# A windowed attention and MLP kernel: the first two batches rebuilt, the global rows split per head, scores and PV reordered

## Chip, cores and metric

One core of a Trainium2 chip. The metric is the device time of one execution in microseconds; the kernel before has a median of 496.06 us over 3 runs (493.28 to 496.7).

## The reference

Shapes: 8 batches, 8 heads, 576 positions, head size 64; model width 512, hidden width 2048; all inputs fp32. Attention with a window of 32 to either side, plus 8 global positions that see all and are seen by all, then a residual MLP with a token mix:

```python
scores = scale * np.matmul(q, k.transpose(0, 1, 3, 2))
mask = (np.abs(pos[:, None] - pos[None, :]) <= 32) | is_global[:, None] | is_global[None, :]
attn = softmax(where(mask, scores, -1e9))        # per batch and head
x = np.matmul(attn, v)                           # heads side by side: (8, 576, 512)
tok = np.einsum('ts,bsd->btd', w_tok, alpha1 * x + beta1)
u = x + lam * tok
out = u + lam * (np.maximum((alpha2 * u + beta2) @ w_ch1, 0.0) @ w_ch2)
```

## The kernel before

The kernel is written out by hand: every engine executes its instructions in the order in which the program emits them, and DMA queues belong to the engine that issues (SP, ScalarE's or POOL's; POOL's convert types).

**A batch of attention.** Heads go in four pairs (hp). `sc_unit(b, hp, u)` is a third of a pair's band scores: three matmuls KT × QP (144 or 128 columns) into a score bank (there are two, banks 3 and 4), Exp on ScalarE to E; the third unit also makes on VectorE PGQ (queries at global positions) and PT (masked band). QP holds Q padded to two halves per pair, with 8 global query columns at each even block of 64; `qpad` and `gcols` copy these in on VectorE from QT and QGT, and `gcols` also places the gathered global keys in KGP. `gk_half` makes the scores of the global keys against all queries (EG, and with the mask GM the rows G). `gq_pv` computes, for the global queries, PGQ × Ve and turns it into RG by three VectorE operations (lines 308 to 310). `pv_x` and `pv_y` compute five tiles of 128 positions: G × RG (one matmul, 130 columns for two heads), then per head PT × Ve and PT × Vo (65 columns each: 64 and the sum); `norm` divides on VectorE into XR, and XL = XR · LA1 follows (on VectorE for batch 0, on POOL for others; LA1 is alpha1 · lam).

**Token mix and MLP.** `tok_tile` multiplies wtT (transposed w_tok) with XL; `finish_u` adds x on VectorE, POOL makes UB = u · alpha2, and a DMA transpose on SP's queue writes it into UT. The MLP runs over nine groups of four tiles (an "S" tile joins the last 64 positions of two batches): 64 matmuls with W1, Relu on ScalarE into HT, 64 matmuls with W2, of 512 columns each: 128 slots. W2 is scaled by lam when it is loaded (`w2_scale`, lines 711 to 715, in group 0), so an output is one VectorE addition, x = bank + x (line 483), and a DMA.

**The order.** `weave` lays attention of batch g+1 over slots 2 to 90 of group g and its token mix over 94 to 114; loads of batch g+2 start at slots 2 to 60 (`prefetch`, K and Q as bf16 by POOL's queue in 256-byte runs), their DMA transposes into KT and QT at 60 to 100 (`xbars`), `qpad` and `gcols` at 116 to 127. Within a batch `attention` (line 437) orders units so:

```python
a = [gk_half(b, 0), gk_half(b, 1)]
...
a += [s[0], w[0], s[1], w[1], w[2], s[2], w[3], w[4]]   # s: scores of pair i, w: PV of pair i-1
if i < HP:
    a.append(gq_pv(b, i))
```

**The first batch** runs ahead of the groups (lines 506 to 706): K and Q are loaded as fp32 in runs of 1 KB (`ld_b0`), cast, and transposed by TensorE one pair at a time between score units; then PV, row sums of w_tok (times ones, for beta1), token mix, bias1 (W1 × beta2). Batch 1 there takes the way of the later batches: `prefetch(1)` at line 674, `xbars(1)`, `qpad`, `gcols` at lines 717 to 721, directly before group 0. POOL multiplies LA1 by lam at line 647, after the loads of line 634.

Of the kernel before, what the change touches and what calls it, by code (L numbers as in the profile page):

```python
# [47 lines left out]
def _consts():  # L48
    p = np.arange(P)
    c16 = np.zeros((P, 64 + 576 + 130), np.float16)  # L50
# [4 lines left out]
    for a in range(2):  # L55
        c16[:, 640 + 65 * a : 705 + 65 * a] = (ab == a)[:, None]
    c16[64:, 640:770] /= GSC
    c16[80, 640:770] = 0
    c16[80, [704, 769]] = EPS_B
    c32 = np.zeros((P, 176), np.float32)  # L60
    c32[:, 48:176] = np.eye(P)
# [727 lines left out]
```

## Time and profile before

| | |
|---|---|
| median of 3 runs | 496.06 us |
| the profiled execution: its time, its span | 495.06 us, 493.3 us |
| TensorE busy | 387.7 us (79%) |
| VectorE busy | 241.4 us (49%) |
| POOL busy | 218.8 us (44%) |
| ScalarE busy | 155.7 us (32%) |
| mean granted TensorE clock (of full speed) | 0.952 |
| moved by DMA | 52.63 MB |

Busy time says how long an engine had an instruction in it; matmuls overlap in a pipeline, so TensorE's share is not a share of its peak. The idle time before an instruction, and what ended it, say more: a stage ends with the wait that ends last in it.

### The profile page before, as it was taken

To read this page: it belongs to the slowest core of one execution; us is meant where nothing else is said; L and a number is where in the kernel's file an instruction comes from. 1 tells how busy PE (TensorE), PEld (TensorE's weight loads), DVE (VectorE), ACT (ScalarE), POOL (GpSimd) and SP (SyncE) were. 2 spreads that over 40 slices of the span, in tenths; PEclk is the share of its full clock that TensorE was granted. 3 is DMA by queue.
4 is the path that set the end of the run, shared out by engine and by line. 5 is a ranking of instruction groups with operands and counts; after the bars stand their busy time and mean duration, and the time that the engine had idled before them with its cause. 6 is when DMAs were issued, how large, how long until landed. Compare 5 with 4: busy or idle time off the path is not lost.

```text
span 493.3 us, 7444 instructions
## 1 busy us (share of the span) xinstructions
PE 387.7 (79%) x2727; PEld 204.8 (42%) x2727; DVE 241.4 (49%) x697; ACT 155.7 (32%) x275; POOL 218.8 (44%) x270
## 2 busy tenths in 40 slices
PE   0336640657897889978998898899889888999995
PEld 0225420333444544544455444444544454444442
DVE  7666620576654556456544555655464555301101
ACT  1242100443105610750076035402640461062440
POOL 6459161266345834854656467546454122500000
PEclk9998585687999999999999999999999999999999
DMA  9999749499269945992599369949965200221102
GB/s 210 211 208 156 34 102 182 90 200 167 42 130 144 114 59 122 154 111 54 122 179 82 68 159 132 72 102 145 142 46 139 76 2 23 64 55 43 44 21 64
DMA packets 179008, 52.63 MB, mean 107 GB/s; under 512 B 166806, under 2 KB 171802, under 8 KB 178972
## 3 DMA queue, kind: packets, MB, share of 16 engines
q0 software_dynamic: 107264, 20.20, 52.0%
q1 hardware_dynamic: 69964, 30.59, 30.0%
q10 hardware_dynamic: 1744, 1.38, 1.0%
q8 instruction: 21, 0.34, 0.3%
q14 instruction: 15, 0.12, 0.1%
HBM read 39.38 MB, written 9.44 MB: 99 GB/s over the span
## 4 chain that ended last, share of the span: by engine, by line
PE 44%; DVE 23%; DMA 10%; issue 8%; SPq 5%; ACT 5%; POOL 3%; POOLq 0%; DVEq 0%; ACTq 0%
PE bank L119 43%; DVE PT L292 4%; DVE QP L216 4%; ACT E L280 3%; DVE PGQ L287 3%; DMA UT<-UB 3%; DMA KG<-in_k_dram,hidx 2%; DVE RG L310 2%; SPq L208 2%; SPq L211 2%; DVE XR L338 2%; DVE RGt L309 2%; DMA XR<-in_moe_w_ch_dram 1%; DVE SR L338 1%; POOL UB L401 1%
## 5 line engine op out<-in xcount | busy, mean ns | idle before, releaser
L119 PE MATMUL bank<-UT,W 128*128 128x512 bf16 x576 | 160.7, 387 | 9.2 <-DMA UT<-UB 7.6
L119 PE MATMUL bank<-W,HT 128*128 128x512 bf16 x576 | 142.5, 379 | 0.0
L470 ACT ACTIVATE HT<-bank,bias 128x512 bf16<-128x512 f32 x144 | 98.9, 687 | 85.3 <-PE bank L119 82.5
L119 PEld LDWEIGHTS <-HT 128*128 128x128 bf16 x576 | 52.0, 98 | 50.6
L361 POOL TENSOR_TENSOR XL<-XR,LA 128x384 bf16<-128x384 f32 x28 | 27.9, 998 | 87.8 <-DVE XR L338 54.8
L401 POOL TENSOR_TENSOR UB<-XR,A 128x512 bf16<-128x512 f32 x32 | 40.5, 1267 | 58.9 <-DMA UT<-UB 25.8
L119 PEld LDWEIGHTS <-W 128*128 128x128 bf16 x640 | 50.8, 99 | 35.9 <-issue 11.0
L119 PE MATMUL bank<-RG,G 128*128 128x130 f16 x160 | 36.0, 226 | 32.7 <-DVE RG L310 32.7
L280 ACT ACTIVATE E<-bank 128x416 f16<-128x416 f32 (+1 forms) x96 | 48.0, 511 | 40.5 <-PE bank L119 40.3
L256 ACT ACTIVATE EG<-bank 128x288 f16<-128x288 f32 (+2 forms) x16 | 6.6, 410 | 168.4 <-PE bank L119 168.3
L119 PEld LDWEIGHTS <-PT 128*128 128x128 f16 x576 | 33.9, 101 | 53.7 <-issue 39.8
L483 DVE TENSOR_TENSOR XR<-bank,XR 128x512 f32<-128x512 f32 x32 | 21.9, 685 | 54.9 <-PE bank L119 54.9
L119 PE MATMUL bank<-XL,wtT 128*128 128x512 bf16 x180 | 44.9, 379 | 0.8 <-ACT wt4o L688 0.8
L335 DVE RECIPROCAL rd<-bank 128x6 f32<-128x6 f32 (+2 forms) x96 | 16.6, 173 | 54.7 <-PE bank L119 54.1
L119 PE MATMUL bank<-Ve,PT 128*128 128x65 f16 x320 | 40.6, 199 | 0.0
L398 DVE TENSOR_TENSOR XR<-bank,XR 128x512 f32<-128x512 f32 x32 | 22.1, 691 | 36.1 <-PE bank L119 36.1
L200 POOL DMA_DIRECT2D Ve<-in_v_dram x40 | 34.7, 876 | 4.4 <-DVE Ve L504 2.2
L119 PEld LDWEIGHTS <-KT 128*128 128x128 bf16 x288 | 25.7, 104 | 23.7 <-issue 5.4
L119 PE MATMUL bank<-QP,KT 128*128 128x144 bf16 (+1 forms) x288 | 34.2, 234 | 1.4 <-ACT E L280 1.4
L216 DVE COPY QP<-QT 64x576 bf16<-64x576 bf16 x56 | 25.0, 446 | 18.7 <-DMA QT<-Qb 18.1
L287 DVE TENSOR_TENSOR PGQ<-E,gqm 128x80 f16<-128x80 f16 x64 | 16.8, 302 | 33.3 <-ACT E L280 33.2
L119 PE MATMUL bank<-Vo,PT 128*128 128x65 f16 x256 | 33.1, 198 | 0.0
(109 smaller groups left out, 394.3 us busy)
## 6 DMA issues: line engine op xcount, KB each, us to landing
out_dram<-XR SPq DMA_DIRECT2D x32, 256.0 KB, 2.2
Vo<-Ve SPq DMA_DIRECT2D x16, 260.0 KB, 3.8
XR<-in_moe_w_ch_dram POOLq DMA_DIRECT2D x8, 512.0 KB, 4.5
Kb<-in_k_dram POOLq DMA_DIRECT2D x28, 128.0 KB, 6.2
Qb<-in_q_dram POOLq DMA_DIRECT2D x28, 128.0 KB, 6.0
Ve<-in_v_dram POOLq DMA_DIRECT2D x24, 128.0 KB, 4.4
W<-in_moe_w_ch_dram POOLq DMA_DIRECT2D x4, 512.0 KB, 16.4
Ve<-in_v_dram POOLq DMA_DIRECT2D x16, 96.0 KB, 4.7
```

Of the source, the lines that this page charges most:

```text
L119: nc.tensor.matmul(out=o, lhsT=l, rhs=r, start=st, stop=sp, skip_group_check=True)
L200: nc.gpsimd.dma_start(out=Ve[b % 2][r0 : r0 + hi - lo, c, :, 0:D], in_=v[b, :, lo:hi, :].rearrange("h p d -> p h d"))
L216: nc.vector.tensor_copy(out=QP[r, hp, a, :, 0:64], in_=QT[r, hp, 0:S].rearrange("p (t j) -> p t j", j=64))
L280: nc.scalar.activation(out=e[:, UOFF[u] : UOFF[u + 1]], in_=ps[:, 0:off], func=AF.Exp, bias=0.0, scale=0.125)
L287: nc.vector.tensor_tensor(out=pg[:, :, c0 : c0 + 16].rearrange("p c (a g) -> p c a g", a=2), in0=gq_in, in1=gq_m, op=ALU.mult)
L292: nc.vector.tensor_tensor(out=bass.AP(pt.tensor, pt.offset + 64 + 128 * par, [p0, [256, n], [1216, 2], [1, 64]]), in0=bass.AP(e.tensor, e. ...
L335: nc.vector.reciprocal(out=rt[r0:r1, 0:m], in_=pv[:, :, 64:65].rearrange("p i o -> p (i o)"))
L361: xl_eng(b).tensor_tensor(out=XL[b % 2][:, 0:3, 128 * hp : 128 * hp + 128], in0=xo, in1=bass.AP(l.tensor, l.offset, [l.ap[0], [0, 3], [1, ...
L398: nc.vector.tensor_tensor(out=x, in0=ps, in1=x, op=ALU.add)
L401: nc.gpsimd.tensor_tensor(out=ub, in0=x, in1=A2, op=ALU.mult)
L470: nc.scalar.activation(out=HT[:, ec, :], in_=st["ps"], func=AF.Relu, bias=bias1[:, ec : ec + 1], scale=1.0)
L483: nc.vector.tensor_tensor(out=x, in0=ps, in1=x, op=ALU.add)
```

## The change

- **Loads.** Batch 1's K and Q come like batch 0's, as fp32 in 1 KB runs (`ld_kq`, `ld_tail`) on SP's queue, half of them behind wtT's DMA transposes. Batch 0's loads go nearly all to SP. The identity for transposes is an own constant.
- **Batch 0** transposes all pairs first, then scores, with fills and mask arithmetic hung between units (`hooks`); QP, XL4, V and other fills go to POOL ahead of the gather; XL of batch 0 goes to POOL; the product of LA1 and lam goes from POOL to VectorE.
- **Batch 0's UT** is made by TensorE: four fp32 transposes per tile, VectorE multiplies by alpha2 out of the bank (`late`). No UB and no DMA transpose for these four tiles.
- **Batch 1** is cast (K on POOL, Q on VectorE) and transposed by TensorE inside group 0: `first_attention(1)` lies over slots 4 to 112, its token mix over 112 to 124. `tr_pair` uses the two score banks.
- **W2** is loaded straight as bf16, unscaled, four DMAs; each output becomes ot = bank · lam, x = ot + x on VectorE.
- **Global rows**: G gets one copy per head of a pair, so G × RG becomes two matmuls of 65 columns; RG is one ScalarE copy with a scale and one VectorE operation on 32 partitions.
- **Order**: a batch's scores of the first pair come ahead of the global keys; s0 and s1 come ahead of the first PV tile; the gather's arithmetic and transposes are spread over slots 44, 56 and 60; `norm` takes one reciprocal for two tiles in `pv_y`.

The core of the diff (other functions keep their computation):

```diff
+    def g_rows():
+        for lo, hi, o in ((0, 512, 0), (512, S, 576)):
+            n = hi - lo
+            e = EG[:, lo:hi]
+            nc.vector.tensor_tensor(
+                out=G[:, :, o : o + n], in0=bass.AP(e.tensor, e.offset, [e.ap[0], [0, 2], [1, n]]), in1=GM[:, :, lo:hi], op=ALU.mult
+            )
...
+    def gk_pair(hp, pss):
+        def f():
+            for hf, t0, nt in ((0, 0, 4), (1, 4, 5)):
+                for a in range(2):
+                    o = pss[hf][:, 0 : 64 * nt].rearrange("p (t j) -> p t j", j=64)
+                    mm(o, KGP[:, hp, :], QP[:, hp, a, t0 : t0 + nt, 0:64], hp == 0 and a == 0, hp == HP - 1 and a == 1)
+            if hp == HP - 1:
+                for hf, q0, n in ((0, 0, 256), (1, 256, 320)):
+                    nc.scalar.activation(out=EG[:, q0 : q0 + n], in_=pss[hf][:, 0:n], func=AF.Exp, bias=0.0, scale=0.125)
+                g_rows()
+        return (0.6, f)
...
-            m2 = C16[:, 640:770]
-            nc.vector.tensor_tensor(out=rg, in0=ps[:, 0:130], in1=m2, op=ALU.mult)
-            nc.vector.tensor_tensor(out=RGt[96:128], in0=ps[96:128, 0:130], in1=m2[96:128], op=ALU.mult)
-            nc.vector.tensor_tensor(out=rg[96:128], in0=RGt[96:128], in1=rg[96:128], op=ALU.subtract)
+            nc.scalar.activation(out=rg, in_=ps[:, 0:130], func=AF.Copy, bias=0.0, scale=C32[:, 36:37])
+            nc.vector.scalar_tensor_tensor(
+                out=rg[96:128], in0=ps[96:128, 0:130], scalar=1.0 / GSC, in1=rg[96:128], op0=ALU.mult, op1=ALU.subtract
+            )
...
         gs = slice(128 * i, 128 * i + 128) if i < 4 else (slice(576, 704) if par == 0 else slice(512, 640))
-        mm(o, G[:, gs], RG[hp % 2], True, False)
         pt = PT[hp % 2]
         for a in range(2):
             oa = o[:, 65 * a : 65 * a + 65]
+            mm(oa, G[:, a, gs], RG[hp % 2][:, 65 * a : 65 * a + 65], True, False)
...
-        return nc.vector if b == 0 else nc.gpsimd
+        return nc.gpsimd
...
+        g, j = PLACE[t]
+        js = slice(128 * j, 128 * j + 128)
+        if t[0] == 0:
+            def tail():
+                for cc in range(4):
+                    nc.tensor.transpose(out=ps[:, 128 * cc : 128 * cc + 128], in_=x[:, 128 * cc : 128 * cc + 128], identity=ident)
+                ab = bass.AP(a2c.tensor, a2c.offset, [a2c.ap[0], [1, 4], [0, 128]])
+                nc.vector.tensor_tensor(out=UT[g % 2][:, :, js], in0=ps.rearrange("p (c t) -> p c t", c=4), in1=ab, op=ALU.mult)
+            late.append(tail)
+            return
         ub = UB[nub[0] % 2]
         nub[0] += 1
         nc.gpsimd.tensor_tensor(out=ub, in0=x, in1=A2, op=ALU.mult)
-        g, j = PLACE[t]
-        nc.sync.dma_start_transpose(out=UT[g % 2][:, :, 128 * j : 128 * j + 128], in_=ub)
+        nc.sync.dma_start_transpose(out=UT[g % 2][:, :, js], in_=ub)
...
-        a = [gk_half(b, 0), gk_half(b, 1)]
+        a = []
         for i in range(HP + 1):
             s = [sc_unit(b, i, u) for u in range(3)] if i < HP else []
             w = pv_x(b, i - 1) + pv_y(b, i - 1) if i > 0 else []
-            if not w:
-                a += s
+            if i == 0:
+                a += s + [gk_half(b, 0), gk_half(b, 1)]
             elif not s:
                 a += w
             else:
-                a += [s[0], w[0], s[1], w[1], w[2], s[2], w[3], w[4]]
+                a += [s[0], s[1], w[0], w[1], w[2], s[2], w[3], w[4]]
...
-                    nc.vector.tensor_tensor(out=x, in0=ps, in1=x, op=ALU.add)
+                    ot = OT[nout[0] % 2]
+                    nout[0] += 1
+                    nc.vector.tensor_tensor(out=ot, in0=ps, in1=LAM, op=ALU.mult)
+                    nc.vector.tensor_tensor(out=x, in0=ot, in1=x, op=ALU.add)
...
+    def cast_k(hp, copy):
+        copy(out=KB0[:, :, 128 * hp : 128 * hp + 128].rearrange("p j (a d) -> p a j d", a=2), in_=KST[:, 2 * hp : 2 * hp + 2, :, :])
+    def cast_q(b, hp, copy):
+        copy(out=QB0[b][:, :, 128 * hp : 128 * hp + 128].rearrange("p j (a d) -> p a j d", a=2), in_=QST[:, 2 * hp : 2 * hp + 2, :, :])
+    def tr_pair(b, hp):
+        def f():
+            kt = KT[b % 2]
+            if b == 0:
+                psq, psk = [banks[i].bitcast(BF16) for i in ((0, 1) if hp % 2 == 0 else (2, 6))]
+            else:
+                psq, psk = sc_ps().bitcast(BF16), sc_ps().bitcast(BF16)
+            hs = slice(128 * hp, 128 * hp + 128)
+            for ps, st_ in ((psq, QB0[b]), (psk, KB0)):
+                for j in range(4):
+                    nc.tensor.transpose(out=ps[:, 128 * j : 128 * j + 128], in_=st_[:, j, hs], identity=identb)
+            if hp == 0:
+                pst = (banks[7] if b == 0 else pv_ps()).bitcast(BF16)
+                for i in range(4):
+                    nc.tensor.transpose(out=pst[:, 128 * i : 128 * i + 128], in_=TSB[:, 128 * i : 128 * i + 128], identity=identb)
+            nc.scalar.copy(out=kt[:, hp, 32:544].rearrange("p (t j) -> p t j", j=4), in_=psk[:, 0:512].rearrange("p (j t) -> p t j", j=4))
+            for a, eng in ((0, nc.vector.tensor_copy), (1, nc.scalar.copy if b == 0 else nc.vector.tensor_copy)):
+                r = slice(64 * a, 64 * a + 64)
+                eng(
+                    out=QP[r, hp, a, 0:8, 0:64].rearrange("p t (u j) -> p t u j", j=4),
+                    in_=psq[r, 0:512].rearrange("p (j t u) -> p t u j", j=4, t=8),
+                )
+            if hp == 0:
+                tv = pst[:, 0:512].rearrange("p (i t) -> p i t", i=4)
+                nc.scalar.copy(out=kt[:, :, 544:608], in_=tv[:, :, 0:64])
+                for a in range(2):
+                    r = slice(64 * a, 64 * a + 64)
+                    nc.vector.tensor_copy(out=QP[r, :, a, 8, 0:64], in_=tv[r, :, 64:128])
+        return (1.2, f)
+    def first_attention(b):
+        pss = [None, None]
+        def hold():
+            pss[0], pss[1] = pv_ps(), pv_ps()
+        def s(hp):
+            return [sc_unit(b, hp, u) for u in range(3)]
+        tail = s(0) + [gk_pair(0, pss)] + s(1) + [gk_pair(1, pss), gk_pair(2, pss), gk_pair(3, pss), gq_pv(b, 0)]
+        if b == 0:
+            a = [tr_pair(b, hp) for hp in range(HP)] + [(0.0, lambda: gcols(b)), (0.0, hold)] + tail
+        else:
+            a = [tr_pair(b, 0), (0.0, lambda: gcols(b)), (0.0, hold), tr_pair(b, 1)] + tail[0:4] + [tr_pair(b, 2)] + tail[4:8] + [tr_pair(b, 3)] + tail[8:]
+        for hp in range(HP):
+            s3 = s(hp + 2) if hp + 2 < HP else []
+            g1 = [gq_pv(b, hp + 1)] if hp + 1 < HP else []
+            a += s3[0:2] + pv_x(b, hp) + pv_y(b, hp) + g1 + s3[2:3]
+        return a
...
+    for c in range(5):
+        load_v(0, c)
...
+    def b0_weights():
+        for t_, src in ((LA1, alpha1), (LAM, lam), (A2, alpha2)):
+            nc.sync.dma_start(out=t_, in_=src.unsqueeze(0).to_broadcast([P, DM]))
+        for r in (64, 0):
+            nc.sync.dma_start(out=LB[r : r + 1, :], in_=beta1.unsqueeze(0))
+        nc.sync.dma_start(out=abr[0:4, :], in_=beta2.rearrange("(c p) -> c p", p=P))
+        nc.sync.dma_start(out=abr[4:8, :], in_=alpha2.rearrange("(c p) -> c p", p=P))
+        nc.vector.tensor_tensor(out=LA1, in0=LA1, in1=LAM, op=ALU.mult)
...
+    def b0_wtok():
+        for tcn in range(5):
+            c0 = 128 * tcn if tcn < 4 else 576
+            nc.sync.dma_start_transpose(out=wtT[:, :, c0 : c0 + 128], in_=WTB[:, tcn, :])
+        nc.sync.dma_start(out=wt4o[64:128, :], in_=wtT[0:64, 4, :])
+    def b1_fills():
+        for c in range(5):
+            load_v(1, c)
+        ld_w1(2)
+        ld_w1(3)
+    def b1_kq(h0, h1):
+        ld_kq(k, KST, nc.sync, 1, h0, h1)
+        ld_kq(q, QST, nc.sync, 1, h0, h1)
+    def cast0(hp):
+        cast_k(hp, nc.scalar.copy)
+        cast_q(0, hp, nc.vector.tensor_copy)
+    def b0_gather():
+        for i in range(2):
+            gather_x(i)
+            gather_tr(0, i)
...
+    hooks = {
+        0: [lambda: cast0(2)],
+        1: [b0_arith, lambda: cast0(3)],
+        3: [b0_gather],
+        4: [b0_masks, lambda: copy_vo(0), b0_weights],
+        9: [b0_gm, b1_fills, lambda: b0_beta(0)],
+        10: [lambda: ld_tail(k, nc.sync, 1, 0), lambda: ld_tail(q, nc.sync, 1, 64), lambda: b1_kq(0, 4), b0_wtok, lambda: b1_kq(4, 8)],
+    }
+    cast0(1)
+    for i, (w, f) in enumerate(early):
+        f()
+        for h in hooks.get(i, []):
+            h()
...
+    for hp in range(HP):
+        cast_k(hp, nc.gpsimd.tensor_copy)
+        if hp == 1:
+            for blk in range(4):
+                nc.gpsimd.dma_start(out=W2[:, 4 * blk : 4 * blk + 4, :], in_=w_ch2[512 * blk : 512 * blk + 512, :].rearrange("(c p) e -> p c e", p=P))
+    b0_beta(1)
...
+    for i, (w, f) in enumerate(token_mix(0)):
+        f()
+        if i > 0:
+            late[i - 1]()
+    late[3]()
...
+    nc.vector.tensor_copy(out=TSB, in_=TST)
+    for hp in range(HP):
+        cast_q(1, hp, nc.vector.tensor_copy)
...
-        if g == 0:
-            slots[0] += [lambda: w2_load(0), lambda: w2_load(1)]
-            for blk in range(8):
-                slots[8 + 7 * blk].append(lambda blk=blk: w2_scale(blk))
         if nb < NB:
             if nb % 2 == 0:
-                def tr(pr=nb // 2):
-                    gather_tr(pr)
-                timed([lambda pr=nb // 2: gather(pr)], slots, 1, 2)
-                timed([tr], slots, 40, 41)
+                pr = nb // 2
+                slots[1].append(lambda pr=pr: gather(pr))
+                slots[44] += [lambda: gather_x(0), lambda: gather_x(1)]
+                slots[56].append(lambda pr=pr: gather_tr(pr, 0))
+                slots[60].append(lambda pr=pr: gather_tr(pr, 1))
...
-        parts = [(attention(g + 1), 2, 90), (token_mix(g + 1), 94, 114)] if g + 1 < NB else []
+        if g == 0:
+            parts = [(first_attention(1), 4, 112), (token_mix(1), 112, 124)]
+        elif g + 1 < NB:
+            parts = [(attention(g + 1), 2, 90), (token_mix(g + 1), 94, 114)]
```

## Rows read from the trace of the kernel before

**Rows 1.** Stages: start:end, length; busy us per engine; TensorE clock, DMA share, GB/s

```profile
66.90:89.10 22.20, 1.01 (x2) 0.14 (x2) 3.98 (x12) 0.00 (x0) 7.58 (x8) 0.58 0.91 168
89.10:150.20 61.10, 48.67 (x314) 24.89 (x314) 37.44 (x99) 17.01 (x30) 30.35 (x38) 0.87 0.80 123
...
196.40:246.10 49.70, 43.67 (x317) 22.87 (x318) 27.24 (x83) 16.68 (x30) 30.36 (x37) 1.00 1.01 110
```

**Rows 2.** Timeline of TensorE: start us, us, instruction [idle before <-releaser]

```profile
89.11 1.14 PE L119 MATMUL bank<-QT,KGP 128*128 128x288 bf16 x4 [13.83 <-DVE KGP L222]
```

**Rows 3.** Timeline of SP's queue, first and last of ten transposes

```profile
70.61 1.26 SPq L208 DMA_TRANSPOSE KT<-Kb  x1
...
82.57 1.22 SPq L211 DMA_TRANSPOSE QT<-Qb  x1
```

**Rows 4.** Groups of TensorE by line, 246.1 to 291.3: busy, mean ns | idle before

```profile
L119 PE MATMUL bank<-RG,G 128*128 128x130 f16 x20 | 4.4, 219 | 2.8 <-DVE RG L310 2.8
...
L119 PE MATMUL bank<-Ve,PGQ 128*128 128x130 f16 x20 | 1.8, 222 | 1.0 <-DVE PGQ L287 1.0
```

**Rows 5.** The same view, 291.3 to 340.9

```profile
L119 PE MATMUL bank<-RG,G 128*128 128x130 f16 x20 | 4.4, 219 | 3.4 <-DVE RG L310 3.4
...
L241 PE MATMUL bank<-C,QGx 128*128 128x128 f32 x1 | 0.3, 330 | 0.7 <-DVE QGx L239 0.7
```

**Rows 6.** Timeline of TensorE in a steady group

```profile
273.94 0.22 PE L119 MATMUL bank<-RG,G 128*128 128x130 f16 x1 [1.26 <-DVE RG L310]
...
291.17 0.66 PE L119 MATMUL bank<-QT,KGP 128*128 128x288 bf16 x4 [0.69 <-DVE KGP L222]
```

**Rows 7.** Timeline of all engines, the first 40 us

```profile
8.79 2.59 POOL L200 DMA_DIRECT2D Ve<-in_v_dram  x3
...
16.40 0.44 DVE L239 TENSOR_SCALAR KGx<-KG,C 128x64 f32<-128x64 f32 x2 [2.05 <-DMA KG<-in_k_dram,hidx]
...
18.11 0.53 SPq L204 DMA_DIRECT2D Vo<-Ve  x1
...
19.96 0.55 SPq L634 DMA_DIRECT2D LAM<-in_moe_lam_dram  x1
...
25.41 12.64 SPq L645 DMA_TRANSPOSE wtT<-HT  x5
...
29.51 1.26 POOL L647 TENSOR_TENSOR LA<-LA,LAM 128x512 f32<-128x512 f32 x1 [8.39 <-DMA LAM<-in_moe_lam_dram]
...
31.02 1.89 DVE L292 TENSOR_TENSOR PT<-E,mask 128x640 f16<-128x640 f16 x2
...
35.30 0.61 PE L576 MATMUL bank<-identb,UT 128*128 128x128 bf16 x4 [0.32 <-ACT UT L569]
```

**Rows 8.** Timeline of TensorE, batch 0's PV and token mix

```profile
41.55 0.22 PE L119 MATMUL bank<-RG,G 128*128 128x130 f16 x1 [1.49 <-DVE RG L310]
41.60 0.19 PE L119 MATMUL bank<-Ve,PT 128*128 128x65 f16 x1
41.63 0.19 PE L119 MATMUL bank<-Vo,PT 128*128 128x65 f16 x1
...
55.73 0.27 PE L119 MATMUL bank<-RG,G 128*128 128x130 f16 x1 [2.66 <-DVE RG L310]
...
60.82 4.48 PE L119 MATMUL bank<-XL,wtT 128*128 128x512 bf16 x20 [0.80 <-ACT wt4o L688]
```

**Rows 9.** Groups by line over the span

```profile
L713 DVE TENSOR_TENSOR W<-XR,LAM 128x512 bf16<-128x512 f32 x16 | 10.9, 725 | 1.9 <-DMA XR<-in_moe_w_ch_dram 1.9
L310 DVE TENSOR_TENSOR RG<-RGt,RG 32x130 f16<-32x130 f32 x32 | 10.8, 336 | 1.1
...
L308 DVE TENSOR_TENSOR RG<-bank,C 128x130 f16<-128x130 f32 x32 | 9.1, 285 | 0.4
```

**Rows 10.** Timeline of VectorE at the start of a steady group

```profile
291.03 0.30 DVE L228 COPY QP<-QGT 128x160 bf16<-128x160 bf16 x2
...
296.39 0.82 DVE L292 TENSOR_TENSOR PT<-E,mask 128x640 f16<-128x640 f16 x2
```

More of the change, by code (lines that the diff above doesn't have):

```diff
@@ L54, in _consts @@
     ab = (p % 16) // 8
[L55 to L61, printed above, removed]
+    oh = ((p >= 64) & (p < 80)) | ((p >= 96) & (p < 112))
+    c32 = np.zeros((P, 40), np.float32)
     c32[:, 0:9] = 64 * np.arange(9)[None, :] - 32 + p[:, None]
@@ L394 @@
     nub = [0]
+    late = []
     def finish_u(t, ps):
@@ L633 @@
-    for t_, src in ((LA1, alpha1), (LAM, lam), (A2, alpha2)):
-        nc.sync.dma_start(out=t_, in_=src.unsqueeze(0).to_broadcast([P, DM]))
-    for r in (64, 0):
-        nc.sync.dma_start(out=LB[r : r + 1, :], in_=beta1.unsqueeze(0))
-    nc.sync.dma_start(out=b2r, in_=beta2.rearrange("(c p) -> c p", p=P))
-    fill(XL4[0], 0.0, nc.gpsimd)
-    fill(XL4[1], 0.0, nc.gpsimd)
-    fill(ones, 1.0, nc.gpsimd)
-    fill(wtT[:, :, 512:576], 0.0, nc.gpsimd)
-    fill(wt4o, 0.0, nc.gpsimd)
-    for tcn in range(5):
-        c0 = 128 * tcn if tcn < 4 else 576
-        nc.sync.dma_start_transpose(out=wtT[:, :, c0 : c0 + 128], in_=WTB[:, tcn, :])
@@ L646, with ld_w1 @@
-    nc.sync.dma_start(out=wt4o[64:128, :], in_=wtT[0:64, 4, :])
-    nc.gpsimd.tensor_tensor(out=LA1, in0=LA1, in1=LAM, op=ALU.mult)
-    for par, r in ((0, 64), (1, 0)):
-        nc.gpsimd.tensor_tensor(out=XL4[par][r : r + 1, :], in0=LB[r : r + 1, :], in1=LAM[r : r + 1, :], op=ALU.mult)
+    def ld_w1(blk):
+        es = slice(512 * blk, 512 * blk + 512)
+        nc.gpsimd.dma_start(out=W1[:, :, es], in_=w_ch1[:, es].rearrange("(c p) e -> p c e", p=P))
+    ld_w1(0)
+    ld_w1(1)
+    nc.vector.tensor_copy(out=identb, in_=ident)
@@ new lines, in b0_beta @@
+    def b0_beta(par):
+        for par, r in ((0, 64), (1, 0))[par : par + 1]:
+            nc.gpsimd.tensor_tensor(out=XL4[par][r : r + 1, :], in0=LB[r : r + 1, :], in1=LAM[r : r + 1, :], op=ALU.mult)
+    def b0_wtok():
[8 more added lines that the diff above has]
+        ld_w1(3)
@@ new lines @@
+    cast0(1)
[3 more added lines that the diff above has]
+            h()
+    psr, psr2 = pv_ps(), pv_ps()
+    for sc in range(5):
+        mm(psr, ones, wtT[:, sc, 0:512], sc == 0, sc == 4)
+    for sc in range(5):
+        mm(psr2[:, 0:64], ones, wtT[:, sc, 576:640], sc == 0, sc == 4)
+    nc.scalar.copy(out=wtT[64:65, 4, 0:512], in_=psr[64:65, :])
+    nc.scalar.copy(out=wtT[64:65, 4, 576:640], in_=psr2[64:65, 0:64])
+    nc.scalar.copy(out=wt4o[0:1, 0:512], in_=psr[0:1, :])
@@ new lines @@
+    nc.scalar.copy(out=wt4o[0:1, 576:640], in_=psr2[0:1, 0:64])
+    for hp in range(HP):
[4 more added lines that the diff above has]
+    b0_beta(1)
+    psb = pv_ps()
+    nc.tensor.transpose(out=psb[:, 0:8], in_=abr, identity=ident[0:8, 0:8])
+    nc.vector.tensor_copy(out=b2c, in_=psb[:, 0:4])
```

329 lines of the change are left out of this document (129 added, 200 removed).

## The prediction

> **What bounds the kernel now.** I read the table of stages first, cut where groups of the MLP end [rows 1]. In the steady part TensorE is busy 43.67 us of a 49.7 us group, but in the 22.2 us between 66.9 and 89.1 it has two matmuls, at a mean granted clock of 0.58 (mostly the lower of its two levels, 1.2 GHz); group 0 then takes 61.1 us at 0.87. So there are two things to look at: the hole before group 0, and what is left idle in each later group.
>
> TensorE's timeline shows how the hole ends [rows 2]: after 13.83 us for KGP, the first instruction of batch 1's attention goes at 89.11, and the rest of group 0 stands behind it. What came late is on SP's queue [rows 3]: ten DMA transposes of batch 1's K and Q, the first at 70.61, the last ending at 83.79, about 1.3 us each, behind four of batch 0's UT. VectorE's Q padding and KGP follow them.
>
> In a steady group the waits are short and repeat. From 246.1 to 291.3 they are 2.8 us for RG and 1.0 for PGQ [rows 4]; the next group, with a shared tile and a gather, has 3.4 for RG and 0.7 for QGx [rows 5]. The timeline adds one for KGP at a group's start, 0.69 at 291.17, and the longest for RG, 1.26, ahead of a batch's last head pair [rows 6]. Over groups 1 to 6, three of either kind, that is 18.6 us for RG, 5.7 for PGQ, 1.4 for QGx and, with five such waits of 0.7 to 1.0, 4.0 for KGP: 29.7 us. They end on the order of VectorE's queue, not on its throughput.
>
> **Part 1, up to the start of group 0.** UT of batch 0 and K, Q of batch 1 no longer need those fourteen DMA transposes. I walk the new order:
> - POOL does its fills (QP's among them), then the gather, then all five V loads. Before, the gather was out at 8.79 and three V loads followed in 2.59 us, with Vo at 18.11 [rows 7]; two more ahead at 0.86 each and a little for the fills put Vo at 20 to 22. LA1 and LAM follow Vo on SP as before, LAM's issue at 22.5 in place of 19.96.
> - The product of LA1 and LAM moves from POOL to VectorE. Before, POOL sat idle 8.39 us for LAM and began at 29.51, 9.55 us after the issue [rows 7], with only its own later work behind it. After, VectorE waits until 22.5 + 9.5 = 32, and behind it stand the first pairs' PGQ and PT, GM and G. The casts and transposes should be done when the gather is in (16.4 before [rows 7], say 17 now); its transposes and column copies take 4 us, the masks 3: VectorE is there at 24. So this is a new wait of 8 us; bounds 0 (LAM early) and 15.
> - From 32: LA1 0.6, PGQ and PT of two pairs 2.2 (0.3 + 0.82 each), GM 1.4, G 1.0: the first PV near 37, against 41.55 [rows 8].
> - Head pairs came every 4.7 us (41.55 to 55.73 is three) [rows 8], with VectorE full. Of that XL (1.1 us) goes to POOL, RG shrinks from three operations of 0.285 to 0.336 us [rows 9] to one of 0.3 behind ScalarE's copy, one reciprocal (0.2) goes: 2.8 us of work, 3.2 with round trips. The last PV ends at 37 + 3 × 3.2 + 1.5 = 48.
> - Row sums of w_tok and their copies took from 57.2 (55.73 and its 1.5 us) to 60.82: 3.5 us, so 51.5. Token mix 4.48 us [rows 8]; sixteen fp32 transposes, 2 to 4 us, I take 2; then the last tile's sum, four transposes and the product with alpha2, 2 us. Group 0 starts at **60**, bounds 52 and 67.
>
> POOL's four casts of K, the four W2 loads and b0_beta(1) stand behind XL there and are needed only inside group 0: W2 from slot 64 on, over 20 us later. Batch 1's K and Q loads stand on SP's queue behind Vo and the weights, half of them also behind wtT; they should land near 52.
>
> **Part 2, group 0.** The group from 196.4 to 246.1, with a shared tile too, takes 49.7 us with some 6 of waits, so 43.7 of work. Added: 36 bf16 transposes at 0.61 us for four [rows 7], start to start about 0.1 each: 3.6 us; the global keys from QP instead of QT, twice the columns, 1.0. Gone: W2's scaling on VectorE. Waits: four times a pair's transposes take both score banks, and the next user waits for ScalarE's and VectorE's copies out, 1.2 us each, 5 us (bounds 0 and 9); RG, 1.5. In all 55 us (49 to 60). Token mix ends at slot 124 instead of 114, so UT of batch 1 comes later: its last tile has about 4.3 us for the sum, POOL's product and a DMA transpose, which need 5 to 6. I put 1 us on group 1.
>
> Group 0 ends at 60 + 55 + 1 = 116 in place of 150.2: **34 us** gained.
>
> **Part 3, groups 1 to 6.** The order becomes s0, s1, PV, and the global keys come after the first pair's scores.
> - RG: 0.6 us of VectorE's chain and 0.2 of reciprocal go, and s1 ahead of PV gives 0.6 us more cover. Waits of 0.7 to 1.0 vanish; a batch's last pair has no s1, so 1.26 becomes 0.4 and its like in the other groups 0.7: 18.6 shrinks to about 4.
> - PGQ: the global keys now lie between, 5.7 goes to 0. QGx is spread over slots, 1.4 to 0. Behind ScalarE's copy of RG stand only Exp and Relu of later units.
> - Against it: the first scores need the global columns of QP, two copies of 0.30 us together which VectorE makes after KGP [rows 10], so 0.3 us later. And each output gets a second operation on VectorE, x = ot + x: a product of two fp32 SBUF operands took 725 ns [rows 9], 0.64 uncontended as I take it; tile 2's stands directly ahead of the Q pads. The wait of about 0.85 at a group's start becomes 1.75: 4.0 turns into 10.5 over six.
> - RG split per head: a 130-column matmul holds TensorE 50 to 55 ns, a 65-column one 31 (41.55, 41.60, 41.63) [rows 8]: 7 ns for each of 160, 1 us.
>
> 29.7 − (4 + 10.5) − 1 = **14 us** gained; bounds 8 and 21.
>
> **Part 4, the end.** The last output waits for the second operation: 0.6 us lost. In groups 7 and 8 the others lie beside matmuls.
>
> **Sum.** Profiled execution 495.06 (span 493.3): −34 − 14 + 0.6 = 447.7. The median of the runs, 496.06, is 1.0 above that execution; rounded, I say **448**.
>
> **A rule against it.** Two PT products took 1.89 us at 31.02 while POOL multiplied, against 0.82 at 296.39 [rows 7, 10]: a VectorE operation with two SBUF operands can lose about 1.1 us beside POOL. The Trainium skill ("SBUF — State Buffer", Who interferes with whom) says that such an operation and a GpSimd one that reads SBUF exclude each other for a whole instruction. By that rule, with which this row agrees, the sum would be rival 1's in place of mine.
>
> **The rivals.**
> 1. *VectorE and POOL block each other.* The change adds 36 additions beside POOL's UB and moves the first batch's XL and casts to POOL. Each group's addition ahead of the pads meets UB: 1.07 more in six groups, 6 us; in the first batch sixteen POOL operations hold VectorE up about 0.4 us each, 6 us: **460**. For it: the stretched PT. Against: few rows show it.
> 2. *The new waits are not there.* LAM lands before VectorE gets to it (−8) and the starts of groups wait less (−4): **436**. Against: the 9.55 us of LAM.
> 3. *Batch 1's K and Q still come late*, the change not doing what it says: they share an SP queue that waits for Vo and wtT. If they land near 89, part 1 is worth nothing: 495 − 14 = **481**. Against: few, long transfers.
> 4. *Slower.* wtT's five DMA transposes now come behind batch 1's first loads on SP; before they held that queue from 25.41 for 12.64 us [rows 7]. The row sums need them at 48; I have them landing at 44 to 47. Beyond 48 each microsecond is one of the total: from about 102 on the kernel is slower by 1%, at 105 it is 448 + 57 = **505**. Against: nothing in the rows makes a transpose wait that long.
>
> **Chances.** Forecast 0.58 (its own range 441 to 455), rival 1 0.17, rival 2 0.12, rival 3 0.05, rival 4 0.05, mixtures within 1% 0.03. So faster by over 1% (about what a measurement of this kernel tells from no change) 0.92, same 0.03, slower 0.05. The range 433 to 468 takes in the forecast and rivals 1 and 2, with most of the bounds of parts 1 and 2.
>
> **What would show it.** No hole in TensorE before group 0, which starts near 60; VectorE idle for LAM between 24 and 32; PV of batch 0 every 3 us; the first scores of groups 1 to 6 waiting 1.5 to 2 us on QP; no wait on PGQ and one short one per group on RG. I am wrong if group 0 waits for loads or banks, or if the waits on RG stay.

## The result and the profile after

The changed kernel takes **454.48 us** (median of four runs, 450.27 to 455.85) against 495.1 us for the kernel before on the same chip: ratio 0.9166, 95% interval 0.9094 to 0.9238. Ratios compare the fast runs of a kernel with the kernel before on the same chip, and a run over 1.5% above the fastest of its kernel is left out, so a ratio below need not follow from the medians. The forecast was 448 with a range of 433 to 468. The profiled execution took 455.32 us with a span of 453.6; the spans differ by 39.7 us. Counted to the start of a group's last output operation on VectorE, group 0 ends at 128.31 in place of 150.19 (21.9 us gained; predicted 34), groups 1 to 6 take 264.4 us in place of 282.8 (18.4; predicted 14), and the tail is 0.6 us longer, as predicted. The sign and the total hold; the split does not.

The stages of the changed kernel (columns as in [rows 1]):

```profile
0.00:45.60 45.60, 20.36 (x222) 16.23 (x222) 28.61 (x98) 16.26 (x33) 27.92 (x45) 0.89 1.47 197
45.60:57.80 12.20, 0.11 (x5) 0.04 (x2) 1.16 (x5) 0.00 (x0) 5.92 (x9) 0.54 1.43 101
57.80:74.50 16.70, 12.64 (x111) 7.05 (x114) 5.94 (x12) 1.46 (x4) 1.81 (x3) 0.70 1.21 212
74.50:131.20 56.70, 49.92 (x392) 27.96 (x399) 35.83 (x93) 22.36 (x43) 32.85 (x41) 0.97 0.95 97
...
217.60:261.60 44.00, 41.18 (x319) 22.62 (x325) 24.74 (x66) 17.95 (x35) 25.00 (x32) 0.96 1.04 122
...
307.40:350.10 42.70, 39.69 (x319) 21.88 (x324) 24.75 (x66) 17.75 (x35) 22.62 (x29) 1.00 1.19 122
```

The hole from 66.9 to 89.1 in [rows 1] is gone, but a new one stands earlier: 12.2 us from 45.6 with 0.11 us of TensorE. Its timeline names the wait:

```profile
34.74 0.22 PE L114 MATMUL bank<-RG,G 128*128 128x65 f16 x1 [3.59 <-DVE RG L316]
...
57.80 0.58 PE L114 MATMUL bank<-wtT,ones 128*128 128x512 bf16 x1 [12.09 <-DMA wtT<-HT]
...
62.71 0.45 PE L114 MATMUL bank<-wtT,ones 128*128 128x64 bf16 x5 [2.62 <-DMA wtT<-HT]
...
64.05 3.83 PE L114 MATMUL bank<-XL,wtT 128*128 128x512 bf16 x10 [0.69 <-ACT wt4o L759]
...
72.26 1.74 PE L114 MATMUL bank<-b2c,W 128*128 128x1 bf16 x64
```

The first PV of batch 0 goes at 34.74 instead of 41.55 [rows 8], the last ends near 45.6, and then the row sums of w_tok wait 12.09 and 2.62 us for wtT. On SP's queue its five DMA transposes stand behind batch 1's tails and first K and Q loads:

```profile
26.33 0.65 SPq L536 DMA_DIRECT2D SR<-in_k_dram  x1
...
30.71 0.40 SPq L531 DMA_DIRECT2D XR<-in_q_dram  x1
31.21 19.40 SPq L715 DMA_TRANSPOSE wtT<-HT  x5
62.80 0.51 SPq L716 DMA_DIRECT2D wt4o<-wtT  x1
```

They are issued 5.8 us later than before and hold the queue 19.40 us, not 12.64 [rows 7]; wt4o, which waits for the last, goes at 62.80. That is 12.2 us after the queue was free again (50.61): a transpose that has left the queue has not yet landed. Before, wt4o went 3.0 us after the queue was free (38.05):

```profile
41.04 0.47 SPq L646 DMA_DIRECT2D wt4o<-wtT  x1
```

In the steady part, TensorE's waits from 131 to 400 us (waited for: us in total, times, longest):

```profile
PE bank L114 <- DVE QP L222: 8.2, 5, 2.1
PE bank L114 <- DVE RG L316: 3.8, 6, 0.7
PE bank L114 <- ACT E L288: 1.0, 4, 0.4
...
PE bank L114 <- DVE PGQ L295: 0.2, 1, 0.2
```

The RG waits of [rows 4 to 6] are down from 18.6 to 3.8 us, one to a group; PGQ and QGx are gone; a wait for QP's global columns stands at the start of five groups.

### The profile page after: what moved, and what is told of

The parts are those of the page before. It is cut to its first block, busy times and chain, and to the rows that moved or that the text cites. A ratio compares the mean times of both kernels' runs of the same rounds, so it can differ in the third digit from the quotient of the medians.

```text
span 453.6 us, 7775 instructions
## 1 busy us (share of the span) xinstructions
PE 383.4 (85%) x2895; PEld 209.8 (46%) x2947; DVE 235.6 (52%) x613; ACT 167.2 (37%) x312; POOL 212.4 (47%) x271
## 4 chain that ended last, share of the span: by engine, by line
PE 62%; DVE 13%; DMA 4%; issue 3%; ACT 2%; POOL 1%; SPq 0%; DVEq 0%; ACTq 0%; POOLq 0%
PE bank L114 61%; DVE QP L210 4%; DMA XR<-in_q_dram 3%; ACT E L288 2%; DVE PGQ L295 1%; DVE OT L503 1%; DVE PT L300 1%; DMA UT<-UB 1%; DVE QP L567 1%; POOL UB L420 1%; DMA Vo<-Ve 1%; DVE XR L348 1%; DVE SR L348 1%; DVE RG L316 1%; DVE XR L405 0%
## 5 line engine op out<-in xcount | busy, mean ns | idle before, releaser
L114 PE MATMUL bank<-UT,W 128*128 128x512 bf16 x550 | 152.6, 382 | 3.3 <-DMA UT<-UB 1.9
L366 POOL TENSOR_TENSOR XL<-XR,LA 128x384 bf16<-128x384 f32 x32 | 31.9, 995 | 88.4 <-DVE XR L348 53.5
L114 PEld LDWEIGHTS <-W 128*128 128x128 bf16 x640 | 50.7, 98 | 29.7 <-issue 2.5
L420 POOL TENSOR_TENSOR UB<-XR,A 128x512 bf16<-128x512 f32 x28 | 35.6, 1273 | 43.7 <-DMA UT<-UB 24.3
L114 PE MATMUL bank<-RG,G 128*128 128x65 f16 x320 | 44.3, 196 | 12.7 <-DVE RG L316 12.6
L503 DVE TENSOR_TENSOR OT<-bank,LAM 128x512 f32<-128x512 f32 x36 | 24.7, 685 | 50.1 <-PE bank L114 50.0
L114 PE MATMUL bank<-Ve,PT 128*128 128x65 f16 x320 | 44.5, 197 | 0.0
L114 PEld LDWEIGHTS <-G 128*128 128x128 f16 x320 | 31.6, 99 | 20.0 <-DVE G L244 3.4
L341 DVE RECIPROCAL rd<-bank 128x6 f32<-128x6 f32 x64 | 11.8, 184 | 53.8 <-PE bank L114 53.7
L405 DVE TENSOR_TENSOR XR<-bank,XR 128x512 f32<-128x512 f32 x32 | 22.0, 688 | 27.7 <-PE bank L114 25.0
L295 DVE TENSOR_TENSOR PGQ<-E,gqm 128x80 f16<-128x80 f16 x64 | 16.3, 294 | 26.0 <-ACT E L288 26.0
L114 PEld LDWEIGHTS <-wtT 128*128 128x128 bf16 x180 | 17.9, 100 | 22.8 <-issue 2.4
## 6 DMA issues: line engine op xcount, KB each, us to landing
XR<-in_q_dram SPq DMA_DIRECT2D x3, 512.0 KB, 10.5
```

The lines of the kernel that those rows point to most:

```text
L114: nc.tensor.matmul(out=o, lhsT=l, rhs=r, start=st, stop=sp, skip_group_check=True)
L295: nc.vector.tensor_tensor(out=pg[:, :, c0 : c0 + 16].rearrange("p c (a g) -> p c a g", a=2), in0=gq_in, in1=gq_m, op=ALU.mult)
L341: nc.vector.reciprocal(out=rt[:, 0 : 2 * n], in_=ps[:, 0 : 130 * n].rearrange("p (i e) -> p i e", e=65)[:, :, 64:65].rearrange("p i o -> p ...
L366: xl_eng(b).tensor_tensor(out=XL[b % 2][:, 0:3, 128 * hp : 128 * hp + 128], in0=xo, in1=bass.AP(l.tensor, l.offset, [l.ap[0], [0, 3], [1, ...
L405: nc.vector.tensor_tensor(out=x, in0=ps, in1=x, op=ALU.add)
L420: nc.gpsimd.tensor_tensor(out=ub, in0=x, in1=A2, op=ALU.mult)
```

## The experiments

Two theories of the lost 12 us: **T1**, the order of SP's queue makes wtT late; **T2**, the DMA engines are busy with W2, whose four loads GpSimd issues while the last transposes are under way:

```profile
49.18 3.05 POOL L765 DMA_DIRECT2D W<-in_moe_w_ch_dram  x4
```

For the gain, the rivals were which of the three rebuilt paths (batch 1's K and Q, batch 0's UT, the steady order and rows) carries it. "From b2c" is the time from bias1's matmuls (72.26 above) to the end of the span: 381.3 us in the changed kernel, where the early waits play no part. Groups 1 to 6 are also measured between issues of their last outputs: 264.4 us (129.75 to 394.13), before 283.5 (150.57 to 434.11). Kernels below that leave these stages as they are show how far one trace can be trusted: from b2c 379.0 to 379.7 us (wtT first, W2 late, LA1 on GpSimd), groups 1 to 6 in 262.8 to 264.7 (these and UT old).

### wtT first on SP

```diff
-  10: [ld_tail(k), ld_tail(q), b1_kq(0, 4), b0_wtok, b1_kq(4, 8)]
+  10: [b0_wtok (transposes), ld_tail(k), ld_tail(q), b1_kq(0, 4), wt4o, b1_kq(4, 8)]
```

> One edit to the changed kernel: wtT's five DMA transposes go out on SP's queue ahead of batch 1's tails and first K and Q loads; the copy wt4o stays where it was. Theory A (the order on SP's queue makes wtT late): from some 26 us on the transposes take as long as before the change, 16 us, wtT lands at 42 to 45, the row sums no longer wait (12.1 and 2.6 us now), group 0 starts near 60 and the time is 454.5 - 13 = 441 us. Theory B (POOL's loads of W1, V and w_tok fill the 16 DMA engines, so the transposes take their 31 us wherever they stand): they start 5 us earlier and land 5 us earlier, 449 us.

445.75 us (444.19 to 446.74), ratio 0.8985 [0.8941, 0.9029].

```profile
49.98 2.29 PE L114 MATMUL bank<-wtT,ones 128*128 128x512 bf16 x5 [1.94 <-DMA wtT<-HT]
...
53.00 0.45 PE L114 MATMUL bank<-wtT,ones 128*128 128x64 bf16 x5 [0.73 <-DMA wtT<-HT]
...
54.35 4.45 PE L114 MATMUL bank<-XL,wtT 128*128 128x512 bf16 x10 [0.69 <-ACT wt4o L761]
```

The waits fall from 14.7 to 2.7 us. Bias1's matmuls start at 63.39, 8.9 us earlier, less than the 12.0 because the last PV also ends 2.3 us later; from b2c it takes 379.0 us. wtT lands at 50 to 53, not at theory A's 42 to 45, and the time lies between the two theories. W2's loads moved too, to 58.38, because GpSimd's casts ahead of them wait for batch 1's K; so this run alone does not part T1 from T2.

### W2's loads behind all four casts

```diff
 for hp in range(HP):
     cast_k(hp, nc.gpsimd.tensor_copy)
-    if hp == 1:
-        (four W2 loads)
+(four W2 loads)
```

> One edit to the changed kernel: the four W2 loads stand on POOL's queue behind all four casts of batch 1's K instead of two, so they go out only when the second half of batch 1's loads is in, after wtT; SP's order is unchanged. Theory W (W2's 4 MB on the 16 DMA engines hold up wtT's last transposes: in the changed kernel W2 goes out at 49.2 and the last transposes, issued from 46.4, land at 62.7; in the run with LA1 on POOL W2 goes at 44.5 and they land at 65.8): wtT lands at 50 to 54, the waits of 12.1 and 2.6 us shrink to 5 or less, 454.5 - 9 = 445 us. Theory S (only the order on SP's queue, behind batch 1's first megabyte): less than 2 us gained, 453 us.

450.75 us (450.21 to 452.44), ratio 0.9108 [0.9051, 0.9164], which overlaps the changed kernel's.

```profile
55.82 2.56 PE L114 MATMUL bank<-wtT,ones 128*128 128x512 bf16 x10 [8.96 <-DMA wtT<-HT]
...
59.48 4.45 PE L114 MATMUL bank<-XL,wtT 128*128 128x512 bf16 x10 [0.91 <-ACT wt4o L759]
```

and on GpSimd

```profile
62.87 3.05 POOL L764 DMA_DIRECT2D W<-in_moe_w_ch_dram  x4
```

W2 now goes at 62.87, after the row sums, and yet they wait 8.96 us; wtT lands at 56.1, not at theory W's 50 to 54. In the changed kernel and those below that are the same up to this point the two waits sum to 7.0 to 16.9 us, so 8.96 tells little of W2's share; that most of the wait stays without W2 speaks for T1.

One comparison parts the two. In this kernel and in the one with wtT first, W2 goes only after the row sums, so up to them the two differ in the order on SP's queue. Token mix starts at 59.48 here and at 54.35 there, and the times are 450.75 and 445.75 us, with intervals that do not overlap: the order by itself is worth some 5 us. For T2 speaks that the last transpose lands 5.0 us after its issue here, against 16.3 in the changed kernel. W2's share in the time stays open: with SP's order unchanged and W2 issued at 44.5 to 52.2, token mix starts between 59.68 and 67.55 in the kernels whose first batch has the new rows, so W2 may cost nothing or 8 us.

### LA1 times lam back on GpSimd

```diff
-        nc.vector.tensor_tensor(out=LA1, in0=LA1, in1=LAM, op=ALU.mult)
+    def b0_la():  # hung behind b1_fills
+        nc.gpsimd.tensor_tensor(out=LA1, in0=LA1, in1=LAM, op=ALU.mult)
```

> One edit to the changed kernel: the product of LA1 and lam goes back from VectorE to POOL. VectorE no longer waits for LAM (5.0 us at 28.8). Theory A (that wait lies beside the longer one for wtT): PV of batch 0 ends 3 to 5 us sooner, the wait for wtT grows by as much, group 0 starts as now, 454 us. Rival (the wait is on the path): 449 to 450 us.

459.57 us (457.57 to 462.75), ratio 0.9272 [0.9218, 0.9327]: no gain, and 5 us above theory A. VectorE's wait for LAM goes, but TensorE only comes earlier to the same wait: 20.47 and 1.78 us for wtT, bias1's matmuls at 76.14. W2's loads go at 44.49 here, and the transposes hold the queue 22.11 us; but the old order below holds it 21.98 with W2 at 49.93, so this says little for T2.

### QP's global columns ahead of KGP

```diff
-timed([lambda hp=hp: qpad(hp) for hp in range(HP)] + [lambda: gcols(nb)], slots, 116, 127)
+timed([lambda: qpad(0), lambda: gcols(nb)] + [lambda hp=hp: qpad(hp) for hp in (1, 2, 3)], slots, 116, 127)
```

(and in `gcols` KGP's copy comes after QP's)

> One edit to the changed kernel, in groups 0 to 6: after the pad of the first pair VectorE copies the global columns into QP and then KGP, and the other three pads come behind. Theory A (the first scores wait for VectorE's queue, 8 us in all over groups 1 to 6, and only one pad and the columns belong to them): the waits of 0.8 to 2.1 us on QP go, 454.5 - 8 = 446 us, perhaps 1 us more where the low clock after such a wait goes too. Rival (another wait takes their place: the key matmuls on KGP, or UT's last tile): less than 3 us gained, 452 us.

451.64 us (445.48 to 456.1), ratio 0.9035 [0.8954, 0.9116]; its trace waits 13.43 and 2.48 us for wtT, and that the spread comes from this wait is likely but not shown, since one run alone left a trace. From b2c it takes 374.4 us, 6.9 less than the changed kernel and 4.6 less than the lowest that is the same there; theory A had 8. The QP waits fall to 0.6 us from 8.2, and 2.4 us come back as waits for a bank that the output's product (OT) has not yet left, because it stands behind the pads.

### One operation per output

```diff
-nc.vector.tensor_tensor(out=ot, in0=ps, in1=LAM, op=ALU.mult)
-nc.vector.tensor_tensor(out=x, in0=ot, in1=x, op=ALU.add)
+nc.vector.tensor_tensor(out=x, in0=ps, in1=x, op=ALU.add)
```

> The changed kernel with the multiplication by lam left out of the output, so that each of the 36 outputs is one VectorE addition again (W2 stays unscaled, so the output lacks lam in its last term). It prices the second operation. Theory A (on the path only where it stands ahead of the pads, 0.7 us in groups 1 to 6, and at the very end): 454.5 - 5 = 449.5 us. Rival (VectorE and POOL block each other, so that the additions cost more all over the groups): 444 us or less. Third (all beside matmuls but the last): 453.8 us.

453.69 us (446.61 to 456.38), ratio 0.9066 [0.898, 0.9153]; the times are no different from the changed kernel's, but its trace waits 16.6 us for wtT. From b2c it takes 373.9 us, 7.4 less (5.1 less than the lowest that is the same there), and groups 1 to 6 take 259.3, 5.1 less: theory A. The QP waits from 75 to 400 us go from 8.2 to 5.4, and the tail is 0.7 shorter. So the second operation is part of the QP wait, not all: the pads ahead of the global columns stay.

### Batches 2 to 7 in the old order; the old rows; both

```diff
-a = []                                          (old order)
+a = [gk_half(b, 0), gk_half(b, 1)]
-a += [s[0], s[1], w[0], w[1], w[2], s[2], w[3], w[4]]
+a += [s[0], w[0], s[1], w[1], w[2], s[2], w[3], w[4]]
...
-nc.scalar.activation(out=rg, ...); nc.vector.scalar_tensor_tensor(out=rg[96:128], ...)   (old rows)
+three VectorE operations by the mask m2, one G for both heads
```

> One part undone: within batches 2 to 7 the order of before (global keys first, then s0, w0, s1, w1, w2, s2, w3, w4); the rest stays. Theory A (order and RG's shorter chain share the gain of groups 1 to 6): RG waits come back to about 0.3 to 0.7 more at three places, PGQ 1.0, KGP 1.5 instead of QP 1.8: group time +1.2 us, so 7 us in six groups, 461 us by the median, and 7 more in the trace from bias1 to the end (381.3 in the changed kernel). Rival (RG's shorter chain alone did it): 1 us or less, 455 us.

> One part undone: G without a copy per head, G x RG as one matmul of 130 columns, RG by three VectorE operations with the two masks as before; order and all else of the changed kernel stay. Theory A (the shorter chain to RG shares the gain): RG waits of 0.2 to 0.5 come back in three places and the last pair waits 1.2 to 1.5 again, minus 0.14 per group for 20 fewer matmuls: +1.2 us per group, 7 to 8 us in six groups and 1 to 2 in the first two batches, 463 us. Rival (the new order covers RG's chain by itself): 1 to 3 us, 456 us.

> The order of scores and PV of batches 2 to 7 and the old RG rows (one G, three operations on VectorE) both as before; alone the first made the trace 4.7 us longer from bias1's matmuls to the end, the second 6.7 us. Theory A (each stands for its own waits): together 11 us, 466 us. Theory B (each covers for the other, which is why undoing one costs less than half of the 18.4 us that groups 1 to 6 gained): together 17 to 19 us, about 472 us, with RG waits of 16 to 19 us in groups 1 to 6.

Order alone 462.99 us (460.12 to 463.69), ratio 0.9324 [0.9262, 0.9386], groups 1 to 6 in 269.1 us. Rows alone 462.47 (456.6 to 463.98), too spread for an interval, groups 1 to 6 in 270.3. Both 476.86 (475.92 to 481.42), ratio 0.9617 [0.955, 0.9683], and groups 1 to 6 in **282.8** us, the kernel before's 283.5. Each undone alone costs 4.7 and 5.9 us, both 18.4. The waits from 131 to 420 us show why. Old order with new rows:

```profile
PE bank L114 <- DVE KGP L216: 6.8, 5, 2.0
PE bank L114 <- DVE PGQ L295: 5.7, 6, 1.0
PE bank L114 <- DVE RG L316: 3.8, 6, 0.7
```

New order with old rows:

```profile
PE bank L118 <- DVE QP L227: 8.1, 5, 2.3
PE bank L118 <- DVE RG L320: 8.0, 8, 1.3
```

Both old:

```profile
PE bank L118 <- DVE RG L320: 15.6, 18, 1.3
PE bank L118 <- DVE KGP L221: 7.2, 5, 2.1
PE bank L118 <- DVE PGQ L297: 5.9, 7, 1.0
```

The RG waits come 6, 8 and 18 times. A shorter chain (new rows) or more scores ahead of PV (new order) each is enough to hide most of them; only where both are missing does nearly every pair wait. What the old order costs beside the new rows are the waits for KGP and PGQ. That is theory B for the groups (the other 4 us of the total lie outside them), and the two edits together are 18.4 of the 19.1 us that the groups gained. The second operation per output costs some 5 us of the same groups, so by this estimate the other edits there (one reciprocal for two tiles, the gather spread out) give about as much back; that was not tested.

### Batch 1's K and Q, and batch 0's UT, the old way

```diff
-b1_kq(0, 4), b1_kq(4, 8), cast_k, cast_q, first_attention(1)   (K and Q old)
+load_kq_std(k, Kb, 1, c), load_kq_std(q, Qb, 1, c); xbars(1), qpad, gcols(1); attention(1)
...
-    if t[0] == 0: (four TensorE transposes, product on VectorE)   (UT old)
+    (product on GpSimd, DMA transpose, as for the other batches)
```

> One part undone: batch 1's K and Q come as before, bf16 in 256-byte runs by POOL's queue, DMA transposes on SP's queue behind wtT and wt4o, pads and column copies on VectorE ahead of group 0, and group 0 carries attention and token mix of batch 1 at the later batches' slots; batch 0's UT by TensorE stays (batch 0's Q is staged in UT instead of Kb). Theory A (batch 1's way through SP and VectorE is what made the hole): the ten transposes come after wtT, group 0's attention waits until 85 to 90 us, the time is 454.5 + 8, 462 us or more. Rival (without batch 0's UT in front the ten transposes lie beside the token mix, and group 0 is 5 us shorter without TensorE's transposes): 450 to 455 us.

> Only batch 0's UT goes the old way: the product with alpha2 on GpSimd, then four DMA transposes on SP, in place of sixteen TensorE transposes and a product on VectorE. Theory A (the queues decide): the products stand on GpSimd behind the casts of K, which wait until about 72 us for batch 1's second half, so UT comes some 8 us after the row sums of w_tok and group 0 starts near 82 us; about 461 us. Theory B (the wait for wtT hides it all): group 0 starts at 75 to 77 us as in the changed kernel; 453 to 456 us.

> Batch 1's K and Q and batch 0's UT both the old way, so that ten DMA transposes of K and Q and four of UT are on SP's queue again; batch 1's K and Q alone made no loss (451.11 us). Theory A (the hole before group 0 comes from the two together, UT's transposes and the ten in one queue behind GpSimd's work): group 0 waits again for KGP or the Q pads, 10 us or more, 465 to 478 us. Theory B (the earlier first batch keeps them apart): the cost of UT's old way alone, 452 to 461 us.

K and Q old: 451.11 us (450.68 to 455.15), ratio 0.9131 [0.9063, 0.9198], no different from the changed kernel. wtT comes first on SP there and the row sums hardly wait, but XL stands on GpSimd behind the loads of K, Q and V:

```profile
45.05 1.24 PE L114 MATMUL bank<-wtT,ones 128*128 128x512 bf16 x5 [0.26 <-DMA wtT<-HT]
...
59.92 3.78 PE L114 MATMUL bank<-XL,wtT 128*128 128x512 bf16 x10 [12.76 <-POOL XL L366]
...
76.46 0.51 PE L114 MATMUL bank<-QP,KT 128*128 128x144 bf16 x3 [5.77 <-DVE QP L222]
```

UT old: 464.99 us (462.34 to 469.58), ratio 0.9379 [0.9315, 0.9443]; group 0 starts at 81.06 (theory A: near 82), after TensorE idled 13.40 us for UT, whose products stand behind GpSimd's casts:

```profile
68.22 1.54 POOL L542 CAST UT<-XR 128x512 bf16<-128x512 f32 x2 [12.94 <-DMA XR<-in_k_dram]
...
70.96 2.89 POOL L420 TENSOR_TENSOR UB<-XR,A 128x512 bf16<-128x512 f32 x2
75.04 2.64 POOL L420 TENSOR_TENSOR UB<-XR,A 128x512 bf16<-128x512 f32 x2 [1.20 <-DMA UT<-UB]
```

Both old: 474.11 us (473.89 to 476.18), ratio 0.9545 [0.9497, 0.9594]. The hole of [rows 2] is back, with ten transposes in one row behind UT's four as in [rows 3]:

```profile
82.60 0.58 PE L114 MATMUL bank<-UT,W 128*128 128x512 bf16 x1 [13.45 <-DMA UT<-UB]
...
100.79 0.51 PE L114 MATMUL bank<-QP,KT 128*128 128x144 bf16 x3 [17.61 <-DVE QP L222]
```

```profile
67.91 12.41 SPq L421 DMA_TRANSPOSE UT<-UB  x4
80.38 1.26 SPq L202 DMA_TRANSPOSE KT<-Kb  x1
...
92.36 1.22 SPq L205 DMA_TRANSPOSE QT<-Qb  x1
```

By theory A, then: the wait of 17.61 us ahead of batch 1's attention needs the two together; with K and Q alone the old way 5.77 are left. With UT on TensorE, batch 1's K and Q may come by DMA transposes and the time stays the same, but only because the wait for wtT goes with it. Against the kernel that has wtT first and the new K and Q (445.75 us, ratio 0.8985 [0.8941, 0.9029]) the old way is 5.4 us slower as it is laid out here, with XL behind the loads on GpSimd, and the intervals do not overlap.

### Both corrections: wtT first, QP's global columns first

> Both corrections at once: w_tok's five DMA transposes ahead of batch 1's first loads on SP's queue (alone 445.75 us), and QP's global columns ahead of KGP with the first Q pad in front (alone 451.64 us; 6.9 us less from bias1's matmuls to the end of the trace). Theory A (two separate places, the savings add): 439 us, with a row sum wait under 3 us and QP waits under 2 us in all. Theory B (an earlier group 0 meets batch 1 not yet ready, so that one saving eats into the other): 443 to 446 us.

**439.82 us** (437.88 to 442.82), ratio 0.8848 [0.8787, 0.8908]; the two savings add, as theory A had it. The row sums wait 3.1 us (theory A: under 3). Bias1's matmuls start at 64.07 and 374.2 us follow. Waits from 119 to 393 us:

```profile
PE bank L114 <- DVE RG L316: 3.8, 6, 0.7
PE bank L114 <- DVE OT L503: 2.4, 2, 1.7
...
PE bank L114 <- DVE QP L221: 0.7, 1, 0.7
```

## Why the prediction held, and where it failed

1. **Part 1, the start of group 0: failed, and rival 4's mechanism is what failed it.** I had wtT landing at 44 to 47 and the row sums at 48. TensorE was ready early (the last PV ended near 45.6), but wtT's first part was there at 57.8 and its last at 62.7: 14.7 us, of which 12.0 went when wtT was put first on SP (W2 then also came behind it; bias1 came 8.9 us earlier). I named the wait in rival 4 and gave it 0.05 because "nothing in the rows makes a transpose wait that long". I had taken the queue's 12.64 us from the row of before; in the new order it held 19.40, from 5.8 us later, and wt4o, which waits for the last transpose, went 12.2 us after the queue was free, not 3.0. That is 5.8 + 6.8 + 9.2 = 21.8 us, from 41.04 to 62.80: the landing of wtT is the term that was mis-sized. With W2 out of the way the order on SP is worth some 5 us; W2's share of the rest stays open. The walk otherwise: LAM made VectorE wait 5.03 us (28.78), not 8; a pair took 3.3 us (predicted 3.2); token mix, transposes and bias1 took 10.5 us where I had 8.5, having left out bias1's matmuls (1.74 us at 72.26). Against the 60 I said, −2.4 (PV), +14.7, +0.1 (row sums 3.6 for 3.5) and +2.0 give 74.4; it is 74.6 (one matmul of group 0 goes at 73.86, the others from 74.61).
2. **Part 2, group 0: right in size, half right in cause.** It took 53.7 us (55 predicted), bank waits 2 us in place of 5, and one 1.25 us wait for UT after it (predicted 1). But I let both rebuilds count for the 34 us. The experiments show that UT on TensorE is worth 10.5 us here (464.99 − 454.48), batch 1's K and Q nothing by themselves in this order of SP's queue and 5.4 once wtT is first, and the two together 19.6 (474.11 − 454.48; 18.8 by the ratios, since the kernel before was slower on that chip).
3. **Part 3, groups 1 to 6: right, a little under.** RG 3.8 us (I said 4), PGQ 0.2 (0), QP 8.2 (10.5); no run measures the loss of 1 us for split RG by itself. Of the 29.7 us of waits 12.2 are left, so the waits account for 17.5 of the 18.4 us that were gained in place of 14. What I did not see is that order and rows stand in for each other: 4.7 and 5.9 us alone, 18.4 together.
4. **Part 4**: 0.6 us, as predicted.
5. **Rival 1, VectorE against GpSimd: there, but small.** The added operation takes 691 ns at best, 785 on the mean of 32 and 1320 at worst, 1603 at worst for the shared tile:

```profile
L504 DVE TENSOR_TENSOR XR<-OT,XR x32: 691/692/1320, 105.9 to 445.3; 128x512 f32<-128x512 f32 x32
...
L504 DVE TENSOR_TENSOR SR<-OT,SR x4: 692/1006/1603, 197.8 to 448.7; 128x512 f32<-128x512 f32 x4
```

 Over 36 of them that is 29.4 us against 36 × 0.69 = 24.8: 4.6 us of VectorE in all. KGP's copies, 0.17 us in batch 0, take 0.36 on the mean. I had priced 12 us on the path. The stretched additions lie beside GpSimd's product UB (the one of 1.32 us at 203.21 beside a product from 202.71 to 203.98), while the one ahead of the pads, which is on the path, takes 0.69 (212.12); and the first batch's pairs took 3.3 us for 3.2. The Trainium skill ("SBUF — State Buffer", Who interferes with whom) says that such an operation contends with a GpSimd instruction that reads SBUF; the 1320 and 1603 ns agree. The stretched PT of [rows 7] had such a product beside it too, which these rows do not show:

```profile
31.23 2.80 POOL L649 TENSOR_TENSOR XL<-LB,LAM 1x512 bf16<-1x512 f32 x2 [0.46 <-DMA LB<-in_moe_beta_dram]
```

6. **Rivals 2 and 3** did not come: the waits on LAM and QP were there, and batch 1's loads did not hold group 0.

The total came near because the errors have opposite signs: 12 us less at the start, 4.4 more in the groups, 7.7 net. To that extent its nearness is luck.

## What to carry to other kernels

When a change makes one stage earlier, list what every consumer in that stage reads and where its producer now stands in each queue; a transfer that was early enough before (wtT) can become the end of the path just by being moved behind loads that nobody needs yet. Two edits that hide the same wait cannot be priced one at a time: undone singly they looked worth 10.6 us, together 18.4. And undo parts in pairs before crediting a rebuild: of the two paths that closed the hole, one was worth 10.5 us by itself, and the other cost nothing to put back as long as wtT came late, and 5.4 us once it did not.
